# First expert's weight sums and three token groups' operand sums on VectorE, attention's buffers closed earlier, a second raw-weight buffer

## The chip, the cores and the metric

The kernel runs on one core of a Trainium2 chip. The metric is the device time of one execution in microseconds; lower is better. The core has a matrix engine (PE in the profile, TensorE), a vector engine (DVE, VectorE), an activation engine (ACT, ScalarE), a general engine (POOL, GpSimd) and a queue engine (SP, SyncE) that issues nearly all DMAs. Each engine executes its own instructions strictly in the order in which the program holds them and waits on semaphores of the others.

## The reference

Three stages follow each other. The first is a gated linear recurrence over 768 steps for 4 batches of 8 heads of width 48; the second multiplies two projections elementwise and applies two more matrices; the third is a sum over four experts, all of them applied to every token.

```python
for t in range(S):
    state = alpha[:, :, t, :, None] * state + einsum('bhd,bhe->bhde', k[:, :, t], v[:, :, t])
    y[:, :, t] = einsum('bhd,bhde->bhe', q[:, :, t], state)
x = y.transpose(0, 2, 1, 3).reshape(3072, 384)
x = ((x @ moe_w1) * (x @ moe_w2)) @ moe_w3 @ moe_w_out          # 384 -> 1024 -> 384
p = probs / (probs.sum(-1, keepdims=True) + 1e-9)
for e in range(4):
    out += p[:, e:e+1] * (relu(x @ w1[e]) @ w2[e])               # 384 -> 1024 -> 384
```

All data are float32. A float32 product is made as three PE products of two-part operands (`mm3`: high by high, low by high, high by low), so each operand exists as a rounded high half, made on ACT, and the remainder, made by a subtraction on DVE or POOL.

## The kernel before

**Attention.** 24 chunks of 128 tokens (6 steps by 4 batches), three to a tile of 384 tokens, eight tiles. Each chunk has two scans on DVE, products on DVE or POOL (`rk`, `rq`), transposes and small products on PE (`kps`, `su`, `yps`), and ends as two-part columns `xt`. The DMA called `pack` moves rows inside `xt`.

**Products** (`products(j, f)`): per tile j and 128 of the 1024 hidden columns f, nine PE products with w1 and nine with w2 (`abps`); ACT copies the first result (`a_sb`), DVE multiplies the second by it (`g_sb`), SP stores it to DRAM (`spilled`). Three PSUM banks serve these and the next step.

**Second projection** (`moe(j)`): SP loads `spilled` into eight buffers `gg`, ACT and DVE split it, and 72 PE products (`xps`) with the folded matrix w3·w_out follow. ACT puts the results into `raw_x`: tiles 2t and 2t+1 make one of four token groups t, in two buffers used in turn.

**Operands of the experts.** The experts' first product runs in a fast block scheme that makes 20 block products of sums in place of 24: the three by two blocks of x become 17 operands (`X_SUMS`, 13 additions), the twelve weight blocks become 20 (`W_SUMS`, 19 additions of 128 columns). `prepare(t)` adds on POOL, makes the high halves on ACT (`x_hi`) and the low halves on DVE or POOL (`x_lo`). For t = 0 the results go straight to the 17 slots `xo` that the expert products read; for t = 1 and 2 they go through five staging buffers (two `stage`, three `ac`) and a DMA to DRAM (`kept`). Group 3 (`last_x`) is made on POOL during the passes 2 to 4 of the experts. `load_a(e, k)` loads half of an expert's first matrix into the one raw buffer `araw`, adds on POOL and splits in pieces of 640 columns (`W_STEPS`) on ACT and DVE into `wa`.

**Expert passes.** 32 passes i in the order expert e, token group t, half k. A pass has 19 steps g (`PARTS`) with 20 times three PE products `hps`, additions on DVE that read the PSUM banks (line 1265), rectified results split by ACT and POOL (`ho`, `ht`), and 72 products `ops` of the pass before. Pass 0 has only its own first `ops`, from step 13 on. The queue reloads a slot of `xo` right behind its last use in a token group.

**Buffers.** `open_e` closes attention's buffers and opens `araw`, one slot `xo`, one `ho` and `stage` in their place; `x_open` takes 16 slots `xo` from the buffers of w1 and w2. Both wait for the last product of tile 7. The tiles `xt` lie among attention's buffers.

**The order.** Up to the first expert pass, a planner (`Plan`) writes the order of every engine: it takes the operations with their dependencies and assumed costs, and an engine that is free takes the ready operation of the smallest due number. The table of `..._DUE` and `..._STEP` numbers ahead of it sets these. From pass 0 on the order is written out by the loop over passes and by `job` lists of (pass, step) at which a piece of background work is issued.

Of the kernel before, what the change touches and what calls it, by code (L numbers as in the profile page):

```python
# [69 lines left out]
W_STEPS = ((0, 0), (0, 5), (1, 0), (0, 10), (1, 5), (0, 15), (1, 10), (1, 15))  # L70
# [264 lines left out]
TILE_DUE = 113275  # L335
CHUNK_DUE = 43206.6
ATT_DUE = -26971.1
START_DUE = -1.29833e+12
START_STEP = 642464
NEXT_DUE = -5.7734e+11  # L340
NEXT_STEP = 9.71164e+06
LOAD_DUE = -2.1073e+12
UNIT_DUE = 11170.6
ZS_DUE = 666271
CHECK_DUE = 6.11715e+06
KT_DUE = -786.104
U_DUE = 22424.3
Z_DUE = -27633.5
M_DUE = 74534.2
KW_DUE = -24366.4  # L350
QP_DUE = -18168.3
HI_DUE = 10353.8
SC_DUE = 527168
IN_DUE = 72261.5
CONV_DUE = 1650.82
CONV_STEP = 23531.8
RAW_DUE = 85566.7
WO_DUE = 1.00473e+07
W3_DUE = 646348
W3_STEP = 3551.85  # L360
WL_DUE = 1.00421e+07
WL_STEP = 50736
XS_DUE = 6.82742e+06
XS_STEP = 10579
X_DUE = 1.40744e+06
X_STEP = 1.15509e+06
G_LEAD = 4.34505e+06
FIRST_DUE = 15730.2
# [96 lines left out]
def gated_attention_moe_kernel(tc, qT, kT, aT, vP, w1, w2, w3T, wo, probs, ew, out):  # L465
# [4 lines left out]
    with tc.manual_schedule(), root:  # L470
# [3 lines left out]
        att_s = ExitStack()  # L474
        apool = att_s.enter_context(tc.tile_pool(name="att", bufs=1, side="right"))
# [47 lines left out]
        def attention(i):  # L523
# [424 lines left out]
        def open_e():  # L948
            att_s.close()
            nonlocal epool, araw  # L950
            epool = root.enter_context(tc.tile_pool(name="e", bufs=1, side="right"))
            araw = epool.tile([128, NW, 128], F32, name="araw")
# [3 lines left out]
            stages.extend(stage[:, n] for n in range(2))  # L956

        def x_open():
            for _ in range(4):
                x = wtile([128, 4, 2, HT], F32R, "xo")  # L960
                xslots.extend(x[:, n] for n in range(4))
            stages.extend(tiles["ac"][:, n] for n in range(3))
# [16 lines left out]

        def load_a(e, k):  # L980

            for f in range(4):
                nc.sync.dma_start(out=araw[:, KD * f:KD * f + KD],
                                  in_=ew[0][e, 4 * k + f].rearrange("p (n t) -> p n t", n=KD))
# [384 lines left out]
```

## Time and profile before

| | us |
|---|---|
| Device time, median of 3 runs (lowest, highest) | 1218.36 (1217.09, 1219.22) |
| Device time of the profiled execution | 1219.27 |
| Its span, first to last instruction | 1217.5 |
| PE busy in it | 1175.2 (97%) |
| DVE busy | 844.2 (69%) |
| ACT busy | 627.5 (52%) |
| POOL busy | 538.6 (44%) |

A PE product of 384 columns is shown with some 0.34 us, but the next one starts 0.17 us later, so PE's busy share hides that it runs a little slower in some stretches than in others; how many products start in a stretch tells more. The engines' busy times in a stretch, the names of what they wait for, and the chain of work that ended last are the other views used below.

### The profile page before, as it was taken

To read this page: it belongs to the slowest core of one execution; us is meant where nothing else is said; L and a number is where in the kernel's file an instruction comes from. 1 tells how busy PE (TensorE), PEld (TensorE's weight loads), DVE (VectorE), ACT (ScalarE), POOL (GpSimd) and SP (SyncE) were. 2 spreads that over 40 slices of the span, in tenths; PEclk is the share of its full clock that TensorE was granted. 3 is DMA by queue.
4 is the path that set the end of the run, shared out by engine and by line. 5 is a ranking of instruction groups with operands and counts; after the bars stand their busy time and mean duration, and the time that the engine had idled before them with its cause. 6 is when DMAs were issued, how large, how long until landed. Compare 5 with 4: busy or idle time off the path is not lost.

```text
span 1217.5 us, 24933 instructions
## 1 busy us (share of the span) xinstructions
PE 1175.2 (97%) x9186; PEld 1148.5 (94%) x9186; DVE 844.2 (69%) x1420; ACT 627.5 (52%) x1238; POOL 538.6 (44%) x610
## 2 busy tenths in 40 slices
PE   5899999999998899999999999999999999999997
PEld 5799999999997888989999999999999999999997
DVE  8898877684158997756668666686576587566573
ACT  4555555443145665544666565566555545434432
POOL 3123222100048884884656432558434357533332
PEclk8999999999999999999999999999999999999999
DMA  8756676342254689595594785775864854844821
GB/s 321 223 176 192 201 229 184 122 160 93 68 181 139 231 301 372 229 356 192 206 336 156 274 300 176 285 282 200 331 240 174 312 192 169 315 144 155 298 79 42
DMA packets 128723, 262.86 MB, mean 216 GB/s; under 512 B 17104, under 2 KB 64720, under 8 KB 128592
## 3 DMA queue, kind: packets, MB, share of 16 engines
q1 hardware_dynamic: 127728, 259.99, 60.9%
q8 instruction: 75, 1.23, 0.4%
q10 hardware_dynamic: 864, 1.18, 0.3%
q14 instruction: 56, 0.46, 0.1%
HBM read 200.56 MB, written 58.20 MB: 213 GB/s over the span
## 4 chain that ended last, share of the span: by engine, by line
PE 85%; DVE 6%; POOL 4%; DMA 2%; issue 2%; ACT 1%; SPq 0%; DVEq 0%; POOLq 0%; ACTq 0%
PE ops L87 11%; PE ops L86 11%; PE ops L88 10%; PE hps L86 9%; PE hps L87 9%; PE hps L88 8%; PE abps L86 6%; PE abps L87 6%; PE abps L88 6%; DVE raw_x L1265 2%; POOL raw_x L966 2%; PE yps L658 2%; POOL araw L987 1%; PE yps L676 1%; PE xps L88 1%
## 5 line engine op out<-in xcount | busy, mean ns | idle before, releaser
L1265 DVE TENSOR_TENSOR raw_x<-hps,raw_x 128x384 f32<-128x384 f32 x416 | 226.8, 554 | 208.0 <-PE hps L88 197.4
L1248 POOL TENSOR_TENSOR ht<-raw_x,ht 128x384 fp32r<-128x384 f32 x227 | 240.9, 1064 | 287.6 <-ACT raw_x L1247 243.1
L87 PE MATMUL ops<-wb,ht 128*128 128x384 f32 x681 | 231.4, 340 | 0.0
L86 PE MATMUL ops<-wb,ht 128*128 128x384 f32 x681 | 230.8, 339 | 0.0
L88 PE MATMUL ops<-wb,ht 128*128 128x384 f32 x681 | 230.6, 339 | 0.0
L1246 ACT ACTIVATE ht<-raw_x 128x384 fp32r<-128x384 f32 x227 | 118.6, 522 | 215.9 <-DVE raw_x L1265 198.6
L86 PE MATMUL hps<-xo,wa 128*128 128x384 f32 x640 | 219.3, 343 | 7.8 <-DVE raw_x L1265 3.6
L87 PE MATMUL hps<-xo,wa 128*128 128x384 f32 x640 | 215.8, 337 | 0.0
L88 PE MATMUL hps<-xo,wa 128*128 128x384 f32 x640 | 215.4, 337 | 0.0
L1265 DVE TENSOR_TENSOR raw_x<-raw_x,hps 128x384 f32<-128x384 f32 x256 | 136.8, 549 | 23.2 <-PE hps L88 23.2
L1247 ACT ACTIVATE raw_x<-raw_x 128x384 f32<-128x384 f32 x256 | 134.6, 526 | 8.1
L86 PEld LDWEIGHTS hps<-xo,wa 128*128 128x128 f32 x640 | 120.4, 188 | 16.3 <-DVE raw_x L1265 9.7
L86 PEld LDWEIGHTS ops<-wb,ht 128*128 128x128 f32 x681 | 128.1, 188 | 0.0
L88 PEld LDWEIGHTS ops<-wb,ht 128*128 128x128 f32 x681 | 127.9, 188 | 0.0
L87 PEld LDWEIGHTS ops<-wb,ht 128*128 128x128 f32 x681 | 127.5, 187 | 0.0
L87 PEld LDWEIGHTS hps<-xo,wa 128*128 128x128 f32 x640 | 120.5, 188 | 0.0
L88 PEld LDWEIGHTS hps<-xo,wa 128*128 128x128 f32 x640 | 120.4, 188 | 0.0
L987 POOL TENSOR_TENSOR araw<-araw 128x128 f32<-128x128 f32 x152 | 78.4, 533 | 59.8 <-DMA araw<-in_ew_dram 45.8
L1265 DVE TENSOR_TENSOR raw_x<-raw_x 128x384 f32<-128x384 f32 x128 | 91.8, 717 | 4.4
L88 PE MATMUL xps<-gg,w3h 128*128 128x384 f32 x192 | 67.1, 349 | 8.1 <-DVE gg L793 8.1
L761 DVE TENSOR_TENSOR g_sb<-abps,a_sb 128x384 f32<-128x384 f32 x64 | 35.4, 553 | 55.4 <-PE abps L88 45.0
L757 ACT ACTIVATE a_sb<-abps 128x384 f32<-128x384 f32 x64 | 31.3, 489 | 75.7 <-PE abps L88 73.2
(127 smaller groups left out, 2278.5 us busy)
## 6 DMA issues: line engine op xcount, KB each, us to landing
xo<-kept SPq DMA_DIRECT2D x255, 384.0 KB, 6.4
partial<-ac SPq DMA_DIRECT2D x72, 192.0 KB, 1.9
ac<-partial SPq DMA_DIRECT2D x72, 192.0 KB, 6.3
spilled<-g_sb SPq DMA_DIRECT2D x64, 192.0 KB, 2.2
gg<-spilled SPq DMA_DIRECT2D x64, 192.0 KB, 3.1
kept<-stage SPq DMA_DIRECT2D x22, 384.0 KB, 3.2
c_raw<-in_w3T_dram SPq DMA_DIRECT2D x16, 512.0 KB, 3.9
raw_x<-in_w3T_dram SPq DMA_DIRECT2D x8, 1024.0 KB, 6.5
```

What stands on the lines that cost most here:

```text
L86: nc.tensor.matmul(out=ps, lhsT=lh, rhs=rh, start=first, stop=False)
L87: nc.tensor.matmul(out=ps, lhsT=ll, rhs=rh, start=False, stop=False)
L88: nc.tensor.matmul(out=ps, lhsT=lh, rhs=rl, start=False, stop=last)
L658: PE.matmul(out=r["y"][rows, p, t], lhsT=Z[rows, p], rhs=r["q"][rows, p, half], start=p == 0, stop=False)
L757: A.activation(out=us["a"], in_=us[0], func=ACTF.Copy)
L761: V.tensor_tensor(out=us["g"], in0=us[1], in1=us["a"], op=ALU.mult)
L966: G.tensor_tensor(out=r[:, dst], in0=r[:, x], in1=r[:, y], op=SIGN[op])
L987: G.tensor_tensor(out=araw[:, dst], in0=araw[:, x], in1=araw[:, y], op=SIGN[op])
L1246: A.activation(out=hh[:, 0], in_=s, func=ACTF.Relu)
L1247: A.activation(out=s, in_=s, func=ACTF.Relu)
L1248: G.tensor_tensor(out=hh[:, 1], in0=s, in1=f32(hh[:, 0]), op=ALU.subtract)
L1265: V.tensor_tensor(out=tmp[:, s], in0=ins[0], in1=ins[1], op=SIGN[op])
```

## The change

- Additions of `prepare(t)` (t = 0, 1, 2), and all low halves there, are on DVE; group 3 stays on POOL. Additions for the first expert's weights are on DVE, those of the three later experts stay on POOL, now one addition per step of a pass where five stood together.
- `xt` gets a pool of its own; `open_e` waits for attention alone, and `x_open` (which takes the buffers of w1 and w2, and that of `xt` for the second half's `wa`) for the last product of tile 7.
- All three groups pass through staging buffers and DRAM: three `ac` for t = 0 and 1, five for t = 2. Seventeen loads bring group 0 into `xo`; its stores in pass 0 are gone.
- The raw weights of a second half have a place of their own: `stage` and the end of `raw_x[1]`.
- `W_STEPS` splits in pieces of 768 and 512 columns. `last_x` takes 16 of the 19 steps of a pass.
- The whole table of due numbers is new, with separate dues for each tile of `moe` and each group of `prepare`.

```diff
-W_STEPS = ((0, 0), (0, 5), (1, 0), (0, 10), (1, 5), (0, 15), (1, 10), (1, 15))
+W_STEPS = ((0, 0, 6), (0, 6, 12), (1, 0, 6), (0, 12, 16), (1, 6, 12), (0, 16, 20), (1, 12, 16), (1, 16, 20))
...
-X_DUE = 1.40744e+06
-X_STEP = 1.15509e+06
...
+X0_DUE = 152927
+X1_DUE = 20086.3
...
+        xtp = root.enter_context(tc.tile_pool(name="xt", bufs=1, side="right"))
+        xt2 = xtp.tile([128, 2, 2, NP, TT], F32R, tag="xt", name="xt")
...
-            araw = epool.tile([128, NW, 128], F32, name="araw")
+            araws.append(epool.tile([128, NW, 128], F32, name="araw"))
...
+            araws.append(f32(stage.rearrange("p b s n -> p (b s n)")).rearrange("p (n t) -> p n t", t=128))
+            wslots.append(epool.tile([128, 2, NW, 128], F32R, name="wa"))
...
-        def x_sum(t, dst, x, y, op):
+        def x_sum(eng, t, dst, x, y, op):
             r = raw_x[t % 2]
-            G.tensor_tensor(out=r[:, dst], in0=r[:, x], in1=r[:, y], op=SIGN[op])
+            eng.tensor_tensor(out=r[:, dst], in0=r[:, x], in1=r[:, y], op=SIGN[op])
...
             for n, (dst, x, y, op) in enumerate(W_SUMS):
-                G.tensor_tensor(out=araw[:, dst], in0=araw[:, x], in1=araw[:, y], op=SIGN[op])
-                if n % 5 == 4:
-                    yield
+                (G if e else V).tensor_tensor(out=raw_a(k2, dst, dst + 1), in0=raw_a(k2, x, x + 1),
+                                              in1=raw_a(k2, y, y + 1), op=SIGN[op])
+                if e or n % 5 == 4:
+                    yield
...
-        opened = add("SP", 0.0, WL_DUE, open_e, att_all, ab_done[j])
+        opened = add("SP", 0.0, WL_DUE, open_e, att_all)
+        x_ready = add("ACT", 0.0, XA_DUE, x_open, opened, ab_done[j])
...
-                    p = add("POOL", pool(HT), due, lambda a=(t, dst, o, y, op): x_sum(*a), writer[dst], writer[o],
-                            writer[y], readers[dst], port=False)
+                    p = add("DVE", dve(HT), due, lambda a=(V, t, dst, o, y, op): x_sum(*a), writer[dst], writer[o],
+                            writer[y], readers[dst])
...
-                on = (("POOL", pool(HT), G) if t and o % 2 else ("DVE", 1.25 * dve(HT), V))
-                q = add(*on[:2], due, lambda t=t, s=dst, to=to, on=on: x_lo(on[2], t, s, to()), p, port=False)
+                q = add("DVE", dve(HT), due, lambda t=t, s=dst, to=to: x_lo(V, t, s, to()), p)
...
+                k = last_keep[m] = add("SP", 0.55, due, lambda t=t, o=o, to=to: x_keep(t, o, to()), q, kib=384)
+                if t == 0:
+                    add("SP", 0.55, XL_DUE + XL_STEP * o, lambda o=o: x_load(0, o), k, x_ready, kib=384)
...
-                job(load_a(e, 0), *((i0 - 2, g) for g in (0, 0, 0, 0, 4, 8, 11, 14)), *((i0 - 1, g) for g in (0, 1, 2, 3, 4, 5, 6, 8)))
-                job(load_a(e, 1), *((i0 - 1, g) for g in (3, 5, 5, 7, 10, 12, 14, 16)), *((i0, g) for g in (4, 5, 6, 7, 8, 9, 10, 12)))
+                for k in range(KO):
+                    job(load_a(e, k), (i0 - 4 + k, 18), *((i0 - 3 + k, g) for g in range(19)),
+                        *((i0 - 1 + k, g) for g in (1, 2, 3, 4, 5, 6, 7, 9)))
...
-                if i == 0 and g < NX:
-                    x_keep(0, g, xslots[g])
-                if 1 < i < 5:
+                if 1 < i < 5 and g not in (5, 11, 18):
                     next(background, None)
```

What the table does is seen in the order. **PE, second projection.** Before, all 576 products `xps` stand in one row behind the last `abps`; the change of one to the other is:

```order
L88 MATMUL abps<-xt,w2h 128x384
L86 MATMUL abps<-xt,w2h 128x384
L87 MATMUL abps<-xt,w2l 128x384
L88 MATMUL abps<-xt,w2h 128x384
L86 MATMUL xps<-gg,w3h 128x384
L87 MATMUL xps<-gg,w3l 128x384
L88 MATMUL xps<-gg,w3h 128x384
```

Now the first `xps` stand behind 729 of the 1152 `abps`, 153 of them in a row, and then a chunk of attention:

```order
L87 MATMUL xps<-gg,w3l 128x384
L88 MATMUL xps<-gg,w3h 128x384
L673 MATMUL yps<-rq,Z_105 64x64 x8
L673 MATMUL yps<-rq,Z_110 64x64 x8
L632 MATMUL su<-rv,kT 64x48 x8
L621 MATMUL su<-rq,rk 64x64 x16
L691 MATMUL yps<-s,rv 64x64 x16
L86 MATMUL xps<-gg,w3h 128x384
L87 MATMUL xps<-gg,w3l 128x384
```

The `xps` are spread in 14 pieces; behind attention's last product there are 216 `abps` and 144 `xps`, and the last piece, 87 `xps` behind the last `abps`, ends at the first `hps`.

**POOL before, DVE now, the first expert's weights.** `rv` and `Z` belong to attention, `araw` are the weight sums, `raw_x` with two names the operand sums. POOL before, from attention's end:

```order
L684 MEMSET rv 128x1
L987 TENSOR_TENSOR araw<-araw 128x128 x19
L966 TENSOR_TENSOR raw_x_4794<-raw_x_4794 128x384 x6
L987 TENSOR_TENSOR araw<-araw 128x128 x5
L966 TENSOR_TENSOR raw_x_4794<-raw_x_4794 128x384 x7
L987 TENSOR_TENSOR araw<-araw 128x128 x14
L972 TENSOR_TENSOR ac<-raw_x_4795,ac 128x384
```

The same weight sums now, on DVE, with `g_sb` of the products between them:

```order
L990 TENSOR_TENSOR ac<-raw_x_3840,ac 128x384
L1014 TENSOR_TENSOR araw<-araw 128x128 x5
L776 TENSOR_TENSOR g_sb<-abps,a_sb 128x384
L1014 TENSOR_TENSOR araw<-araw 128x128 x10
L776 TENSOR_TENSOR g_sb<-abps,a_sb 128x384
L1014 TENSOR_TENSOR araw<-araw 128x128 x4
L808 TENSOR_TENSOR gg<-gg 128x384 x2
L776 TENSOR_TENSOR g_sb<-abps,a_sb 128x384
```

POOL now holds no sum between attention's last chunk and pass 0. **SP around pass 0.** Before, group 0 is in its slots and is stored from them:

```order
L975 DMA kept<-ac 128x768 x2
L975 DMA kept<-xo 128x768 x17
L1006 DMA braw<-in_ew_dram 128x384 x4
L978 DMA xo<-kept 128x768 x17
L975 DMA kept<-stage 128x768 x2
```

Now it is loaded, among the last loads of `gg`:

```order
L779 DMA spilled<-g_sb 128x384
L800 DMA gg<-spilled 128x384 x3
L996 DMA xo<-kept 128x768 x2
L779 DMA spilled<-g_sb 128x384
L800 DMA gg<-spilled 128x384 x4
L996 DMA xo<-kept 128x768 x2
L800 DMA gg<-spilled 128x384
L1035 DMA braw<-in_ew_dram 128x384 x4
L996 DMA xo<-kept 128x768 x13
L1035 DMA braw<-in_ew_dram 128x384 x4
L996 DMA xo<-kept 128x768 x17
```

The first 17 rows `xo<-kept` are new; the stores of group 0 stand earlier, between the loads of `gg`.

## Rows read from the trace of the kernel before

**Rows 1.** Page, busy time of engines; page, the span in 40 slices.
```profile
PE 1175.2 (97%) x9186; PEld 1148.5 (94%) x9186; DVE 844.2 (69%) x1420; ACT 627.5 (52%) x1238; POOL 538.6 (44%) x610
...
DVE  8898877684158997756668666686576587566573
POOL 3123222100048884884656432558434357533332
```

**Rows 2.** Windows: from:to, length, busy (instructions) of PE, PEld, DVE, ACT, POOL; clock, DMA share, GB/s.
```profile
0.00:45.20 45.20, 27.53 (x674) 23.52 (x674) 37.36 (x68) 23.60 (x49) 12.66 (x17) 0.85 0.85 289
45.20:336.90 291.70, 290.64 (x3710) 282.99 (x3711) 203.67 (x327) 137.57 (x301) 51.76 (x72) 1.00 0.51 161
336.90:453.40 116.50, 106.46 (x579) 100.65 (x577) 94.92 (x100) 65.85 (x141) 89.41 (x92) 0.99 0.63 214
453.40:474.00 20.60, 18.98 (x95) 17.72 (x96) 16.93 (x30) 11.01 (x23) 9.54 (x10) 0.92 0.97 378
474.00:1217.50 743.50, 731.55 (x4133) 723.66 (x4131) 491.35 (x897) 389.46 (x724) 375.22 (x420) 1.00 0.63 229
```

**Rows 3.** Timeline of PE, products without a wait: start, duration, what.
```profile
305.77 0.33 PE L86 MATMUL abps<-xt,w1h 128*128 128x384 f32 x1
...
308.89 0.33 PE L86 MATMUL abps<-xt,w1h 128*128 128x384 f32 x1
```

**Rows 4.** Instructions of tile xps: duration ns min/median/max, first to last start us.
```profile
L86 PE MATMUL xps<-gg,w3h x192: 335/336/525, 337.0 to 452.1; 128*128 128x384 f32 x192
```

**Rows 5.** Waits of PE, 336.9 to 453.4: total us, times, longest.
```profile
PE xps L88 <- DVE gg L793: 8.1, 10, 2.0
PE xps L86 <- ACT raw_x L823: 1.3, 2, 0.9
```

**Rows 6.** Chain that ended last, 366 to 405: start, us, what (the longest pieces).
```profile
375.23 1.30 POOL raw_x L966
376.60 7.32 POOL raw_x L966 x6
```

**Rows 7.** Groups on POOL, 336.9 to 453.4: count, busy, mean ns, idle before.
```profile
L966 POOL TENSOR_TENSOR raw_x<-raw_x 128x384 f32<-128x384 f32 x39 | 48.3, 1249 | 13.9 <-ACT raw_x L823 9.8 <-DVE stage L972 1.9 <-DVE xo L972 1.0
L987 POOL TENSOR_TENSOR araw<-araw 128x128 f32<-128x128 f32 x38 | 23.4, 634 | 43.1 <-DMA araw<-in_ew_dram 41.8
```

**Rows 8.** Groups on DVE, 336.9 to 453.4.
```profile
L793 DVE TENSOR_TENSOR gg<-gg 128x384 fp32r<-128x384 f32 x56 | 56.5, 1053 | 10.5 <-ACT gg L789 10.4
L972 DVE TENSOR_TENSOR xo<-raw_x,xo 128x384 fp32r<-128x384 f32 x17 | 13.9, 837 | 7.9 <-ACT xo L969 7.8
```

**Rows 9.** Group on DVE, 210 to 336.9.
```profile
L793 DVE TENSOR_TENSOR gg<-gg 128x384 fp32r<-128x384 f32 x8 | 4.1, 551 | 0.7 <-ACT gg L789 0.7
```

**Rows 10.** Group on DVE, whole span: the two-input operation of 96 columns.
```profile
L1092 DVE TENSOR_TENSOR p_sb<-p_sb,p_sum 128x96 f32<-128x96 f32 x1 | 0.3, 257 | 0.0
```

**Rows 11.** Groups on ACT, 336.9 to 453.4: high halves into the staging buffers.
```profile
L969 ACT ACTIVATE ac<-raw_x 128x384 fp32r<-128x384 f32 x19 | 9.5, 517 | 3.3 <-POOL raw_x L966 2.1 <-DMA kept<-ac 1.0
L969 ACT ACTIVATE stage<-raw_x 128x384 fp32r<-128x384 f32 x14 | 7.2, 520 | 9.2 <-POOL raw_x L966 6.3 <-DMA kept<-stage 2.9
```

**Rows 12.** DMA issues: count, KB each, median us from issue to landing.
```profile
kept<-ac SPq DMA_DIRECT2D x20, 384.0 KB, 3.4
```

**Rows 13.** Waits of PE, 0 to 60.
```profile
PE abps L86 <- DMA xt<-xt: 2.4, 1, 2.4
...
PE abps L87 <- DVE w2l L95: 1.4, 1, 1.4
```

**Rows 14.** Waits of PE, 480 to 560.
```profile
PE hps L86 <- ACT raw_x L1263: 2.3, 3, 1.2
```

**Rows 15.** Waits of PE, 560 to the end.
```profile
PE hps L86 <- DVE raw_x L1265: 2.3, 4, 0.7
```

**Rows 16.** Chain that ended last, 820 to 841, a change of expert.
```profile
829.16 1.21 POOL araw L987 x2
```

More of the change, by code (lines that the diff above doesn't have):

```diff
@@ L334 @@
 MM = 0.174
[L335 to L364, printed above, removed]
-X_DUE = 1.40744e+06
-X_STEP = 1.15509e+06
-G_LEAD = 4.34505e+06
-FIRST_DUE = 15730.2
+TILE_DUE = 145435
+CHUNK_DUE = 72150.5
+ATT_DUE = -6421.33
+START_DUE = -731.082
+START_STEP = 42665.8
+NEXT_DUE = -2467.26
+NEXT_STEP = 3757.1
+LOAD_DUE = 10481.4
+UNIT_DUE = 18928.8
+ZS_DUE = 20051.4
+CHECK_DUE = 862129
+KT_DUE = -22247.7
+U_DUE = -9258.47
+Z_DUE = -11294.3
+M_DUE = 21097.1
+KW_DUE = -14986.1
+QP_DUE = 78185.4
+HI_DUE = -1118.42
+SC_DUE = 20341.1
+IN_DUE = -2696.97
+CONV_DUE = 576.798
+CONV_STEP = 29364.4
+RAW_DUE = 62795
+WO_DUE = 2.37049e+06
+W3_DUE = -139285
+W3_STEP = 27551
+WL_DUE = 2.5277e+06
+WL_STEP = -139182
+XS_DUE = 78249.6
+XS_STEP = 202041
+XT_DUE = -68590.4
+XT_STEP = 187420
+XU_DUE = 23006.6
+XU_STEP = 1.68451e+06
+X0_DUE = 152927
+X1_DUE = 20086.3
+X2_DUE = -3995.65
+X3_DUE = -5402.66
+X4_DUE = 601929
+X5_DUE = 174157
+X6_DUE = 931289
+X7_DUE = 2.01771e+06
+XA_DUE = 1.47361e+06
+XL_DUE = 1.12115e+07
+XL_STEP = 121092
+G_LEAD = 862071
+FIRST_DUE = 21070.3
 EARLY = 3
@@ L961, in x_open @@
                 xslots.extend(x[:, n] for n in range(4))
-            stages.extend(tiles["ac"][:, n] for n in range(3))
-        def x_sum(t, dst, x, y, op):
+            w = xtp.tile([128, 4 * NP * TT], F32R, tag="xt", name="wa")
+            wslots.append(w[:, :2 * NW * 128].rearrange("p (s n c) -> p s n c", s=2, n=NW))
+        def x_sum(eng, t, dst, x, y, op):
             r = raw_x[t % 2]
-            G.tensor_tensor(out=r[:, dst], in0=r[:, x], in1=r[:, y], op=SIGN[op])
+            eng.tensor_tensor(out=r[:, dst], in0=r[:, x], in1=r[:, y], op=SIGN[op])
         def x_hi(t, slot, to):
@@ L1026, in step @@
                     gen["g"] = load_a(0, k)
-                    for _ in range(3):
-                        next(gen["g"])
                 next(gen["g"], None)
@@ L1032, in gated_attention_moe_kernel @@
             for m in (5, 5, 5, 4):
-                prev = add("POOL", m * 0.52, due + 2, step, prev, port=False)
-            for lo, _ in W_STEPS:
-                prev = add(*(("DVE", dve(640)) if lo else ("ACT", act(640))), due + 2, step, prev)
+                prev = add("DVE", m * dve(128), due + 2, step, prev)
+            for lo, s0, s1 in W_STEPS:
+                n = 128 * (s1 - s0)
+                prev = add(*(("DVE", dve(n)) if lo else ("ACT", act(n))), due + 2, step, prev, x_ready if k else None)
             wl_last = prev
-        x_ready = None
-        kept_ops = []
+        last_keep = [None] * 3 + [opened] * 2
         def prepare(t):
+            made = 0
             writer = {s: [] for s in range(NT)}
```

56 lines of the change are left out of this document (31 added, 25 removed).

## The prediction

> **What bounds the kernel now.** I read the busy shares and the 40 slices first, then the windows by stage, then PE's waits and the chain in the windows where PE falls behind. PE is busy for 97% of the span [rows 1], so a gain can come only from stretches in which PE's products stand further apart than they can. Without a wait, 18 products take 308.89 - 305.77 = 3.12 us, 0.1733 us each [rows 3]. Against that pace the five windows [rows 2] tell where the slack is:
>
> - 45.2 to 336.9 (attention and products): PE busy 290.64 of 291.70 us. Nothing to gain, though DVE is at 70%.
> - 336.9 to 453.4 (second projection alone): 576 products `xps`, three times the 192 of [rows 4], need 576 x 0.1733 = 99.8 us and take 116.5. **16.7 us are lost here.**
> - 453.4 to 474 (pass 0): some 94 products started, 16.3 us, in 20.6 us: about 4.3 us lost, at a granted clock of 0.92.
> - 0 to 45.2: PE is busy for 27.53 us at a clock of 0.85; this is the start.
> - 474 to the end: PE busy 731.55 of 743.50 us; the waits named there are 2.3 and 2.3 us [rows 14, 15].
>
> In the second window PE waits for the low half of `gg` on DVE, 8.1 us in ten waits [rows 5]; the rest of the 16.7 us are shorter gaps and the slow clock behind them. The chain there runs through POOL [rows 6]: 39 operand sums of 1249 ns and 38 weight sums of 634 ns are 48.3 + 23.4 = 71.7 us [rows 7], and POOL is busy for 89.41 of 116.5 us [rows 2]. POOL also slows DVE: the same `gg` operation takes 551 ns while POOL rests [rows 9] and 1053 ns here [rows 8].
>
> **The change part by part.** The sum is made against the profiled execution, 1219.27 us; the median of the three runs is 0.9 us lower, so the result is brought down by that.
>
> *Sums to DVE, second projection spread.* POOL's 71.7 us of sums, and 15 low halves, leave it. On DVE the 39 operand sums take 39 x 0.551 = 21.5 us if they cost what the two-input operation of the same size costs with POOL at rest [rows 9]; a weight sum of 128 columns has no row there: it lies between 257 ns for 96 columns [rows 10] and 551 ns for 384 [rows 9], and I take 290 ns, a ninth of the way (32 of 288 columns), so 11.0 us. DVE gains back 56 x (1.053 - 0.551) = 28.1 us on `gg` [rows 8, 9] and 17 x (0.837 - 0.551) = 4.9 us on the first low halves; 15 more low halves cost it 8.3 us. Net 21.5 + 11.0 + 8.3 - 28.1 - 4.9 = about +8 us on 336 us of DVE work before pass 0 [rows 2]. The work up to pass 0 takes PE some 437 us: DVE, with 344 us, is at 79% there. PE's order is what gives the gain: `xps` no longer stand in one row at the end but in 14 pieces between products and chunks, and behind attention's last product PE still holds 216 + 144 products, 62.4 us, to cover what follows it: the raw weights' DMA, 38 sums (11 us), their splits (8 pieces, 8.0 us before) and group 2's sums and halves (30 x 0.551 = 16.5 us). So the 16.7 us can go. They will not go wholly: 153 `xps` in a row need `gg` reloaded behind themselves, as before. The first 29 us of the old row (337 to 366) had no such wait while `gg` took 551 ns on DVE, so the lower bound of what stays is 0; the upper is the 8.1 us for `gg` with the 1.3 us for `raw_x` [rows 5], 9.4. I take 3, nearer to the lower, since POOL no longer slows DVE. **-13.7 us.**
>
> *The planner's new order at the start.* One conversion moves ahead of the third chunk's scans, and `xt` of that chunk, on which the first product waits through `pack`, is one row earlier on DVE. The waits there are 2.4 us for the `xt` DMA and 1.4 us for `w2l` [rows 13]: 3.8 us either way is the bound; I take **-1 us**.
>
> *Operands of group 0 through DRAM.* 17 loads of 384 KB (6.7 MB) can start only when the last product of tile 7 has freed w1's buffers, and 87 `xps` (15.1 us) stand between that and pass 0. With the 5 last loads of `gg` and 4 of `braw` (1.8 MB) it is 8.5 MB, 22.4 us at the 378 GB/s that the window of pass 0 reached [rows 2]. Pass 0 takes one operand per step, the 13th about 7 us in, 22 us behind that last product; by then 6.9 MB must have landed, 18.2 us and a landing. It just fits. **0**, with up to +10 if the rate is the mean 229 GB/s of the last window [rows 2]: 30 us for the 13th. The stores of group 0 move under attention, where the DMA share is 0.51 [rows 2], and cost nothing there.
>
> *Pass 0 itself* is paced by DVE as before. **0.**
>
> *Passes 2 to 4.* POOL makes group 3 beside its own halves; PE waits 2.3 us there [rows 14]. The same work now stretches over 48 steps instead of 47 in a row. It takes about half: **-1.2 us**, bounds -2.3 and 0.
>
> *Changes of expert.* A change has POOL sums in its chain [rows 16], then splits on DVE; PE waits 2.3 us in four places [rows 15]. Single sums per step take POOL out of it; the splits stay and become longer pieces. **-0.8 us**, bounds -2.3 and +1.
>
> Sum: -13.7 - 1 + 0 - 1.2 - 0.8 = -16.7; 1219.27 - 16.7 - 0.9 = 1201.7, say **1202 us**.
>
> *A rule against it.* The same `gg` operation costs 0.50 us more with POOL busy for 77% of the time than with POOL at rest [rows 2, 8, 9], and in the stretch from 45.2 to 336.9 POOL is busy for 18% (51.76 of 291.7). Scaled, that is 0.12 us more for each of the 39 + 38 + 51 operations put there, 15 us of DVE time, and DVE goes from 79% to 82%: no wait for PE. The Trainium skill, SBUF — State Buffer, section "SBUF: two separate sides", says that VectorE with two SBUF inputs and GpSimd share a port pair as an exclusive lock, and that the loser blocks for the whole of the other's instruction. By that rule each meeting would cost DVE up to a whole POOL product of attention instead of a share, and attention's own `rk` and `rq` would be held up in turn; that is the second rival's mechanism.
>
> **The rivals.**
>
> *Operands late for pass 0.* For it: the loads are not covered by more than 2 us in the working above. Against it: the window of pass 0 did reach 378 GB/s. Price +5 to +10: 1207 to 1212.
>
> *DVE becomes the bound under attention.* DVE is at 89% or more in several slices of the first 200 us [rows 1], and the moved operations come on top, slowed by POOL. If half of the 16.7 us comes back as PE's waits for `g_sb` or `xt`: 1210, range 1207 to 1216. Against it: the sums come after most of the weight conversion, where DVE rested before.
>
> *Slower: staging blocks ACT.* Groups 0 and 1 now have three staging buffers instead of none and five. A high half must wait until the store three tiles back has landed: 3.4 us [rows 12] after halves of 0.52 [rows 11] and 0.55 us. ACT stands still up to 3.4 us per three tiles, 34 tiles make 11 such turns, 37 us, and behind the waiting half on ACT stand the copies `a_sb` that free PE's banks. Three banks cover 27 products, 4.7 us, so a single turn costs nothing. Once each turn costs PE over 1.5 us (16.7 / 11) the kernel is no faster; at the full 3.4 it is 37 - 16.7 = 20 us slower, 1239. Before, ACT waited for such stores 1.0 + 2.9 us in all [rows 11], and the order puts copies between most of the halves, which speaks against it.
>
> *More than forecast.* The start gives its 3.8 us and nothing stays of the stalls: 1219.27 - 0.9 - 16.7 - 3.8 - 2 = 1195.
>
> **How the numbers follow.** Forecast (1195 to 1207) 0.60; operands late 0.12; DVE bound 0.13; more than forecast 0.04; within 0.2% of before (all given back) 0.04; slower, by staging or another wait in the new order, 0.07. A measurement of this kernel can tell about 0.2%, 2.4 us, from no change. The first two rivals end below 1215.9, so faster is 0.60 + 0.12 + 0.13 + 0.04 = 0.89, cut to 0.87 because the second reaches to 1216; same 0.05, slower 0.08. The range leaves out the case below the forecast, the dearest part of the second rival and what is slower: 1195 to 1213.
>
> **What would show it.** Right: pass 0 starts near 439 us instead of 453.4; `gg` takes some 0.55 to 0.7 us on DVE; POOL nearly empty from attention's end to pass 0; PE's waits for `gg` below 3 us; no wait of `hps` for a DMA. Wrong: waits of `hps` for `xo` DMAs in pass 0 (first rival), of `abps` for `g_sb` or `a_sb` between 45 and 340 us (second and third), or a later first `abps`.

## The result and the profile after

Before: 1218.69 us (median of 4, 1217.09 to 1219.22). After: **1197.20 us** (median of 4, 1196.44 to 1198.84). The ratio is 0.9828, with a 95% interval from 0.9811 to 0.9845. The forecast of 1202 was 4.8 us too high; the range, 1195 to 1213, holds the time. The profiled execution of after took 1197.35 us against 1219.27, so 21.9 us have to be found in the two traces.

The page of after, with busy time by engine and the 40 slices of VectorE and POOL (before: [rows 1]):

```profile
PE 1167.1 (98%) x9186; PEld 1149.3 (96%) x9186; DVE 829.2 (69%) x1513; ACT 627.4 (52%) x1238; POOL 445.1 (37%) x517
...
DVE  8898788966665856667677656667666587576563
POOL 2133321010000006776744434744433655433332
```

POOL has lost 93 us, and ahead of the slice in which pass 0 starts five slices in a row stand at 0. VectorE, which took the sums over, is not busier than before (829.2 against 844.2 us): its own operations became shorter. The windows of after, the first two cut at the times of [rows 2] and the others around its own pass 0; columns are from:to, length, busy time of PE, PEld, DVE, ACT, POOL, then granted clock, DMA share and GB/s:

```profile
0.00:45.20 45.20, 27.79 (x673) 23.90 (x673) 37.76 (x64) 23.02 (x48) 13.01 (x17) 0.85 0.81 281
45.20:336.90 291.70, 290.08 (x3556) 283.45 (x3555) 230.24 (x386) 158.77 (x352) 52.87 (x68) 1.00 0.63 201
336.90:440.00 103.10, 102.29 (x735) 101.19 (x733) 64.37 (x142) 46.09 (x94) 0.26 (x4) 1.00 0.73 254
440.00:460.60 20.60, 19.13 (x105) 18.07 (x106) 13.55 (x26) 11.76 (x25) 9.09 (x9) 1.00 0.61 223
460.60:1195.50 734.90, 727.85 (x4123) 722.68 (x4121) 483.25 (x896) 387.72 (x721) 369.88 (x420) 1.00 0.63 228
```

The third window is the point. It was 116.5 us long with PE busy for 106.46 at a clock of 0.99; now PE is busy for 102.29 of 103.10. The two windows do not hold the same work, since the `xps` now start at 250 us; the stretch that can be compared runs from the first `abps` to the first `hps`, in the table below. The groups on VectorE from 230 to 440 us (count, busy time, mean ns, then idle time before) show what became of the operations of [rows 7, 8]:

```profile
L808 DVE TENSOR_TENSOR gg<-gg 128x384 fp32r<-128x384 f32 x64 | 33.5, 554 | 31.0 <-ACT gg L804 30.9
...
L984 DVE TENSOR_TENSOR raw_x<-raw_x 128x384 f32<-128x384 f32 x39 | 20.8, 554 | 2.6 <-ACT raw_x L838 2.0
...
L1014 DVE TENSOR_TENSOR araw<-araw 128x128 f32<-128x128 f32 x38 | 9.7, 289 | 2.5 <-DMA araw<-in_ew_dram 1.9
```

`gg` fell from 1053 to 554 ns, an operand sum from 1249 on POOL to 554, a weight sum from 634 to 289. Waits of PE from 60 to 440 us and from 440 to 560 us (total us, times, longest):

```profile
PE yps L691 <- POOL rv L699: 0.3, 1, 0.3
...
PE hps L86 <- DVE raw_x L1294: 1.2, 1, 1.2
PE hps L86 <- ACT raw_x L838: 0.6, 1, 0.6
```

Nothing is left of [rows 5] or [rows 14]. Only the start is worse. Waits of PE from 0 to 60 us in after:

```profile
PE yps L673 <- DVE xt L710: 6.8, 4, 2.8
...
PE yps L691 <- DVE s L683: 4.5, 3, 2.3
```

The waits of [rows 13] are gone, but the wait for `xt` is three times as long as it was in before, while that for `s` is the same. In before, same window:

```profile
PE yps L676 <- DVE s L668: 4.5, 4, 2.2
...
PE yps L658 <- DVE xt L695: 2.2, 2, 2.0
```

The first `abps` starts at 40.84 instead of 38.80 us.

Where the 21.9 us are, with a pass counted from its first `hps` product to the next pass's (60 products each; a pass without a wait takes 23.20 us):

| stretch | before | after | difference |
|---|---|---|---|
| start to first `abps` | 38.80 | 40.84 | +2.0 |
| first `abps` to first `hps` | 414.60 | 399.25 | -15.35 |
| passes 0 and 1 | 37.94 | 35.90 | -2.0 |
| passes 2 to 4 | 73.62 | 69.80 | -3.8 |
| changes of expert: passes 6 to 8, 14 to 16, 22 to 24 | 215.80 | 212.70 | -3.1 |
| last pass and end | 42.25 | 42.65 | +0.4 |

### The profile page after: what moved, and what is told of

The parts are those of the page before. It is cut to its first block, busy times and chain, and to the rows that moved or that the text cites. A ratio compares the mean times of both kernels' runs of the same rounds, so it can differ in the third digit from the quotient of the medians.

```text
span 1195.5 us, 24960 instructions
## 1 busy us (share of the span) xinstructions
PE 1167.1 (98%) x9186; PEld 1149.3 (96%) x9186; DVE 829.2 (69%) x1513; ACT 627.4 (52%) x1238; POOL 445.1 (37%) x517
## 4 chain that ended last, share of the span: by engine, by line
PE 95%; DVE 3%; DMA 1%; issue 0%; POOL 0%; SPq 0%; ACT 0%; DVEq 0%; POOLq 0%
PE ops L87 11%; PE ops L86 11%; PE ops L88 11%; PE hps L86 9%; PE hps L87 9%; PE hps L88 9%; PE abps L86 6%; PE abps L87 6%; PE abps L88 6%; PE xps L86 3%; PE xps L88 3%; PE xps L87 3%; PE yps L673 2%; PE yps L691 1%; PE wps L86 1%; PE wps L88 1%
## 5 line engine op out<-in xcount | busy, mean ns | idle before, releaser
L1277 POOL TENSOR_TENSOR ht<-raw_x,ht 128x384 fp32r<-128x384 f32 x227 | 238.1, 1051 | 274.5 <-ACT raw_x L1276 222.2
L1294 DVE TENSOR_TENSOR raw_x<-raw_x 128x384 f32<-128x384 f32 x128 | 88.6, 692 | 4.4
L1277 POOL TENSOR_TENSOR ho<-raw_x,ho 128x384 fp32r<-128x384 f32 x29 | 30.7, 1060 | 105.0 <-DMA xo<-kept 71.4
L86 PE MATMUL abps<-xt,w2h 128*128 128x384 f32 x192 | 66.0, 344 | 0.0
L86 PE MATMUL abps<-xt,w1h 128*128 128x384 f32 x192 | 65.9, 343 | 0.0
```

The costliest lines, as they stand in the source:

```text
L86: nc.tensor.matmul(out=ps, lhsT=lh, rhs=rh, start=first, stop=False)
L1277: G.tensor_tensor(out=hh[:, 1], in0=s, in1=f32(hh[:, 0]), op=ALU.subtract)
L1294: V.tensor_tensor(out=tmp[:, s], in0=ins[0], in1=ins[1], op=SIGN[op])
```

## The experiments

In the table the third column is the stretch from the first `abps` to the first `hps`, the fourth from there to the end of the span; both are of the profiled execution. Times with one run are single executions. Where the expectations say first product or expert product, the `abps` are meant; a combine is one of the additions that read the PSUM banks of the `hps`, and a turn is the step of a pass at which a piece of background work is issued.

| kernel | time, us (runs) | `abps` to `hps` | `hps` to end |
|---|---|---|---|
| before | 1218.69 (4) | 414.60 | 764.14 |
| after | 1197.20 (4) | 399.25 | 755.45 |
| after again | 1196.26 (5) | 398.83 | 755.42 |
| after, all sums on POOL | 1199.59 (4) | 402.18 | 755.57 |
| before, sums on VectorE | 1205.14 (4) | 402.28 | 762.65 |
| after, operand sums alone on POOL | 1196.56 (1) | 399.65 | 756.05 |
| after, second projection in one row | 1222.53 (1) | 418.37 | 761.73 |
| after, attention's buffers closed late | 1222.96 (1) | 401.92 | 778.30 |
| after, no steps left out in passes 2 to 4 | 1201.34 (1) | 399.56 | 759.55 |
| after, later weight sums timed three ways | 1202.13 (1) | 399.79 | 759.77 |
| after, one raw-weight buffer, old turns | 1198.42 (1) | 398.07 | 758.96 |
| after, start first | 1196.22 (5) | 400.32 | 755.31 |
| after, start first and earlier turns | 1192.73 (5) | 399.17 | 753.78 |
| after, start mixed and earlier turns | 1198.31 (4) | 403.61 | 755.02 |

### Engine or order: four kernels

**After with the sums on POOL**, every other engine's row untouched:

```diff
-                (G if e else V).tensor_tensor(out=raw_a(k2, dst, dst + 1), ...
+                G.tensor_tensor(out=raw_a(k2, dst, dst + 1), ...
-                    p = add("DVE", dve(HT), due, lambda a=(V, t, dst, o, y, op): x_sum(*a), ...
+                    p = add("DVE", dve(HT), due, lambda a=(G, t, dst, o, y, op): x_sum(*a), ...
```

> The changed kernel with its order left as it is, but the 39 operand sums of the first three groups and the 38 weight sums of the first expert emitted on POOL instead of VectorE. Theory (the spreading is the gain: the operand tiles come out between the expert products, where neither engine is waited for): first hps within 2 us of the changed kernel's 440.1, total 1197 to 1200. Rival (the engine is the gain: POOL's sums slow VectorE's low halves of gg down and end late): gg on VectorE 0.7 to 1.0 us instead of 0.55, TensorE waits of 5 to 12 us before 440, first hps at 446 to 453, total 1203 to 1211.

Measured: 1199.59 us, ratio to before 0.9841 (0.9812 to 0.9869); first `hps` 2.1 us later than after's, at 442.19, just outside the theory's 2 us. With the second projection spread, PE hardly feels POOL's sums. What it feels is one place near 400 us. Waits of PE (336 to 447) and of ACT (392 to 404), then windows with the granted clock in the third column from the end:

```profile
PE abps L86 <- ACT a_sb L772: 1.8, 1, 1.8
...
ACT wa L1026 <- POOL araw L1014: 3.9, 1, 3.9
ACT stage L987 <- DMA kept<-stage: 3.5, 1, 3.5
...
402.00:406.00 4.00, 3.15 (x11) 3.15 (x12) 4.00 (x4) 3.46 (x8) 4.00 (x3) 0.65 0.14 49
406.00:410.00 4.00, 3.65 (x19) 3.33 (x18) 4.00 (x5) 1.43 (x3) 2.66 (x3) 0.93 0.50 197
```

ACT stood 3.5 us at a high half whose staging buffer was not yet stored and 3.9 us at a piece of the first expert's weights whose sums POOL had not made; `a_sb`, which frees a bank, stood behind them, and PE waited 1.8 us. Behind that wait the granted clock was 0.65 and 0.93 in the two windows, in part the lower of its two levels (1.2 instead of 2.4 GHz): 4 x 0.35 + 4 x 0.07 = 1.7 us more. The move of the sums is the only edit taken back here: the spread order, the earlier close and the new way of the operands all stay.

**Before with the sums on VectorE**, its order and its one row of `xps` kept:

```diff
-                G.tensor_tensor(out=araw[:, dst], ...
+                (G if e else V).tensor_tensor(out=araw[:, dst], ...
-            G.tensor_tensor(out=r[:, dst], in0=r[:, x], in1=r[:, y], op=SIGN[op])
+            (V if t < NT2 - 1 else G).tensor_tensor(out=r[:, dst], in0=r[:, x], in1=r[:, y], op=SIGN[op])
```

> The kernel before, its order and its one row of xps kept, but the operand sums of the first three groups and the first expert's weight sums emitted on VectorE. Theory (spreading): the wait of xps for gg (8.1 us before) goes down by half at most, first hps at 446 to 453 (before 453.4), total 1211 to 1219. Rival (engine): gg on VectorE at 0.55 us, no wait for gg above 2 us, first hps at 441 to 444, total 1206 to 1210. Passes 3, 4, 8, 16 and 24 stay as long as before on both, since nothing of them is changed.

Measured: 1205.14 us, ratio 0.9893 (0.9867 to 0.992); first `hps` at 439.74. The theory of spreading falls: without any spreading, 12.3 of the 15.35 us are there. Group `gg` on VectorE, 336 to 440 us; PE's wait for it; and the window after that wait:

```profile
L793 DVE TENSOR_TENSOR gg<-gg 128x384 fp32r<-128x384 f32 x56 | 33.7, 621 | 5.8 <-ACT gg L789 5.6
...
PE xps L88 <- DVE gg L793: 1.1, 2, 1.0
...
406.00:410.00 4.00, 3.83 (x13) 3.52 (x14) 2.98 (x6) 2.55 (x5) 1.01 (x1) 0.67 0.87 269
```

The wait for `gg` fell from 8.1 to 1.1 us as `gg` fell from 1053 to 621 ns. Of the 3.0 us that it still lacks, 2.7 are again one short wait, 1.0 us, with a slow clock behind it: 0.67 in the window shown and 0.90 in the next, 4 x 0.33 + 4 x 0.10 = 1.7 us. Pass 0 is short as well (15.89 us, before 17.57, after 15.73), while passes 3, 4 and 8 stay long (24.38, 25.79, 25.09).

**After with the operand sums alone on POOL** (only the second edit of the first diff):

> The changed kernel with the 39 operand sums of the first three groups on POOL and the first expert's weight sums left on VectorE. Theory (with the spreading, what the sums on POOL cost came of ACT's 3.9 us wait for the weight sums, and the operand sums' engine costs nothing): first product to first hps within 0.6 us of the changed kernel's 399.25, no low granted clock between 336 and 440. Rival (the operand sums cost by themselves): 401 to 402.5 from first product to first hps, as with both on POOL (402.2), and a wait of TensorE over 1 us between 390 and 420.

Measured: 399.65 us from first `abps` to first `hps`, after 399.25. The window 336 to 440 has the full clock, though POOL is busy for 20.62 us there:

```profile
336.00:440.00 104.00, 102.56 (x735) 101.14 (x735) 61.96 (x124) 46.84 (x95) 20.62 (x21) 1.00 0.73 254
```

So, once the second projection is spread, the operand sums' engine costs nothing that one execution shows. What both kinds of sums together cost on POOL then falls, by subtraction, to the first expert's weight sums, for which ACT stood 3.9 us; a kernel with those alone on POOL was not run.

**After with the second projection in one row** (the due numbers of the eight tiles made late):

```diff
-X0_DUE = 152927
...
-X7_DUE = 2.01771e+06
+X0_DUE = 1.40744e+06
...
+X7_DUE = 9.49307e+06
```

> The changed kernel with its sums on VectorE, but the due numbers of the second projection's eight tiles made late, so that its 576 products stand in one row behind the first projection's last product, as in the kernel before. Theory (the engine of the sums and the spreading each give nearly the whole gain, and what is left over is one short wait with a low clock behind it, as in the kernel before with the sums on VectorE): first hps 2 to 4 us after the changed kernel's 440.1, with the granted clock under 0.8 for some us after a wait of xps for gg; total 1199 to 1202. Rival (the early close of attention's buffers changes this, so that one row costs nothing or much more): first hps within 1 us of 440.1, or more than 6 us after it.

Measured: first `hps` at 459.00, 18.9 us after after's and 5.6 after before's. The theory's 2 to 4 us are wrong; this is the mechanism of the prediction's third rival. Waits of PE (336 to 460) and of ACT (330 to 460); then the chain that ended last (start, us, what); then a window:

```profile
PE xps L86 <- ACT raw_x L838: 4.7, 1, 4.7
PE xps L88 <- DVE gg L808: 4.4, 3, 2.2
PE xps L86 <- ACT gg L804: 2.0, 3, 1.1
...
ACT ac L987 <- DMA kept<-ac: 19.1, 26, 2.1
...
432.93 3.53 DMA kept<-ac
...
437.69 4.46 DMA kept<-ac
...
442.67 0.48 ACT raw_x L838
...
444.00:448.00 4.00, 4.00 (x14) 4.00 (x14) 3.51 (x7) 2.63 (x6) 0.00 (x0) 0.50 0.77 304
```

All the high halves of groups 0 and 1 fall into the row of `xps`; with three staging buffers ACT waits 19.1 us for stores, the copies that free PE's banks stand behind, and after PE's 4.7 us wait the clock is at its lower level for 4 us (0.50). The waits shown are 11.1 us, and the granted clock, 0.97 from 336 to 440 us and 0.83 from 440 to 460, costs 104 x 0.03 + 20 x 0.17 = 6.5 more: 17.6 of the 18.9. The chain shows the stores behind the longest wait; that they are behind the others as well is argued. In the kernel before with VectorE's sums, whose first group needs no store, no wait of ACT for a store is among the nine longest of this stretch; that this alone lets it bear one row is argued, not shown, since early close and due numbers differ as well.

### Closing attention's buffers when attention ends

```diff
-        opened = add("SP", 0.0, WL_DUE, open_e, att_all)
+        opened = add("SP", 0.0, WL_DUE, open_e, att_all, ab_done[j])
```

> The changed kernel, but attention's buffers are closed only after the last expert product of the first projection, as in the kernel before, so that the first expert's weights and two of the five staging buffers come after it. Theory (the early close lets VectorE do the weight sums, some 19 us of VectorE and ACT work with their low halves, before the last products): these fall into the last 15 us before pass 0 and behind it, first hps at 444 to 455 instead of 440.1, total 1201 to 1212. Rival (TensorE has enough of the second projection left behind the last product to cover them): first hps within 1.5 us of 440.1, total within 1 us of 1197.2.

Measured: 1222.96 us, 11 us beyond the expected band. First `hps` comes only 2.7 us later, but pass 0 lasts 38.40 us instead of 15.73, at a mean granted clock of 0.72. Waits of PE, 440 to 480, and of ACT, 430 to 475; then DMA issues from 425 to 460 (KB each, median us to landing):

```profile
PE hps L86 <- ACT raw_x L1292: 14.9, 1, 14.9
PE hps L86 <- ACT wa L1026: 4.6, 1, 4.6
...
ACT stage L987 <- DMA kept<-stage: 15.6, 4, 11.2
...
xo<-kept SPq DMA_DIRECT2D x17, 384.0 KB, 7.9
...
araw<-in_ew_dram SPq DMA_DIRECT2D x8, 192.0 KB, 5.7
```

The raw weights are now loaded in the same 35 us as the 17 operands: a load of an operand takes 7.9 us, and the chain of waits has the second half's weights landing at 459.2. VectorE's weight sums wait for them with low halves of group 2 behind; ACT waits 11.2 us for the store of such a half, and the first copy out of PSUM, on which PE waits 14.9 us, stands behind that. The early close is what keeps these two loads apart.

### Passes 2 to 4

```diff
-                if 1 < i < 5 and g not in (5, 11, 18):
+                if 1 < i < 5:
```

> The changed kernel, but the sums and halves of the last group run at every step of passes 2 to 4 again, as in the kernel before (19 steps in a pass instead of 16). Theory (the three steps left out give the combines on VectorE room): passes 3 and 4 go from 23.20 us back to 24.3 to 25.8 each, total +2 to +4 us over the changed kernel. Rival (something else shortened them, such as VectorE's backlog of operand work carried over from the start of the passes): passes 3 and 4 stay within 0.3 us of 23.2, total within 0.6 us.

Measured: passes 3 and 4 back at 24.46 and 25.78 us (before 24.57 and 25.76), every other pass within 0.5 us of after's. The three steps left out are the whole gain there. Waits of ACT from 499 to 550 us in this kernel, and of PE from 480 to 560:

```profile
ACT stage L987 <- POOL raw_x L984: 9.1, 4, 2.7
...
PE hps L86 <- ACT raw_x L1292: 2.5, 3, 1.2
```

A high half on ACT waits for POOL's sum of the step before (9.1 us; in after 3.3), with the copy out of PSUM that PE needs behind it. The waits that PE names, 2.5 us, are less than the 3.8 us that the two passes lose: short gaps around them are not named.

### Changes of expert

**Three timings of the sums**, one for each later expert:

```diff
-                    job(load_a(e, k), (i0 - 4 + k, 18), *((i0 - 3 + k, g) for g in range(19)),
+                    late, bursts = e > 1, e != 2
+                    gs = [g for g in (0, 5, 10, 15) for _ in range(5)][:19] if bursts else range(19)
+                    job(load_a(e, k), (i0 - 4 + late + k, 18), *((i0 - 3 + late + k, g) for g in gs),
```

> The changed kernel with the weight sums of the later experts timed three ways: second expert in bursts of five at the same early pass; third expert single but one pass later, so that they end just ahead of the weights' conversion; fourth expert in bursts and late. In the changed kernel passes 8, 16 and 24 last 23.67 us each, in the kernel before 24.73, 24.74 and 24.90. Theory (the early end counts, since VectorE's low halves of the weights no longer wait for POOL): pass 8 within 0.2 us of 23.67, passes 16 and 24 at 24.2 to 25. Rival (the bursts count, since they hold VectorE's combines up): passes 8 and 24 at 24.2 to 25, pass 16 within 0.2 us of 23.67.

Measured: pass 8 (bursts, early) 23.63; pass 16 (single, late) 27.33; pass 24 (bursts, late) 23.67. Bursts cost nothing, and lateness alone does not either, against the expectation for pass 24. In pass 24 the last sum ended 0.8 us after the pass began; in pass 16 it ended 6.0 us in, after the conversion's first turn on ACT. The rows of pass 16 (POOL, then ACT) and PE's wait in it:

```profile
809.06 0.46 POOL L1014 TENSOR_TENSOR stage<-raw_x,stage 128x128 f32<-128x128 f32 x1
...
809.55 0.84 ACT L1026 ACTIVATE wa<-stage 128x768 fp32r<-128x768 f32 x1 [2.84 <-POOL stage L1014]
...
PE hps L86 <- ACT raw_x L1294: 2.4, 1, 2.4
```

The kernel before has the same wait of ACT in its pass 16, on the buffer that its halves shared:

```profile
830.40 0.74 ACT L997 ACTIVATE wa<-araw 128x640 fp32r<-128x640 f32 x1 [3.66 <-POOL araw L987]
...
839.37 0.82 DVE L995 TENSOR_TENSOR wa<-araw,wa 128x640 fp32r<-128x640 f32 x1
840.10 1.24 DVE L1265 TENSOR_TENSOR raw_x<-hps,raw_x 128x384 f32<-128x384 f32 x2
```

Its conversion then ends 18 us into the pass, and its last low half stands on VectorE right ahead of a combine that PE waits for.

**One raw buffer with the old turns:**

```diff
-            k2 = e and k
+            k2 = 0
-                for k in range(KO):
-                    job(load_a(e, k), (i0 - 4 + k, 18), ...
+                bursts = [[g for g in gs for _ in range(5)][:19] for gs in ((4, 8, 11, 14), (10, 12, 14, 16))]
+                job(load_a(e, 0), (i0 - 2, 0), *((i0 - 2, g) for g in bursts[0]), *((i0 - 1, g) for g in (0, 1, 2, 3, 4, 5, 6, 8)))
+                job(load_a(e, 1), (i0 - 1, 7), *((i0 - 1, g) for g in bursts[1]), *((i0, g) for g in (4, 5, 6, 7, 8, 9, 10, 12)))
```

> The changed kernel with one raw-weight buffer for the later experts and the sums in bursts of five at the turns of the kernel before, the second half's in the pass just ahead of its conversion. Theory (POOL's sums then end some 8 us into passes 8, 16 and 24, and ACT's conversion of the weights waits for them with the combines behind it): passes 8, 16 and 24 at 24.5 to 25 us instead of 23.67, passes 7, 15 and 23 at 23.3, total +1.5 to +3.5 us over the changed kernel. Rival (the change of experts is shorter for another reason, such as the larger pieces of the conversion): passes 8, 16 and 24 within 0.3 us of 23.67, total within 1 us.

Measured: passes 8, 16, 24 at 25.36, 24.83, 24.45; passes 7, 15, 23 at 23.3; 3.5 us more than after from first `hps` to the end (the total, 1198.42 in one execution, hides it by a first `hps` 2.4 us earlier). Pass 8 of this kernel on VectorE:

```profile
630.33 1.48 DVE L1024 TENSOR_TENSOR wa<-araw,wa 128x512 fp32r<-128x512 f32 x1
631.73 0.55 DVE L1294 TENSOR_TENSOR raw_x<-hps,raw_x 128x384 f32<-128x384 f32 x1
```

PE's longest wait for a combine in this kernel's later passes, 2.0 us, is for the one in the second line. So the second raw buffer pays by letting the conversion come early in the pass. How much of it is the sums' end and how much the later turns 4 to 12 was not taken apart.

### The start, and earlier turns

**Attention's first six chunks first:**

```diff
-START_DUE = -731.082
-START_STEP = 42665.8
-NEXT_DUE = -2467.26
-NEXT_STEP = 3757.1
+START_DUE = -1e9
+START_STEP = 642464
+NEXT_DUE = -1e8
+NEXT_STEP = 9.7e6
```

> The changed kernel with four numbers of its table so altered that the first six chunks of attention stand ahead of the weight conversion again, as in the kernel before; from the seventh chunk on every engine's row of instructions is that of the changed kernel. Theory (the later start of the first expert product, 40.8 against 38.8 us, comes of the weight conversion's instructions among the first chunks on VectorE): first product at 37.4 to 39, first hps at 437 to 438.5, total 1 to 3 us under the changed kernel's 1197.2. Rival (the start differs from execution to execution by as much as 2 us whatever the order): first product at 40 or later, total within 0.6 us of 1197.2.

Measured: first `abps` at 38.79, as the theory has it, but first `hps` at 439.11, 1.0 us ahead of after instead of 1.6 to 3: around the first `abps` PE again waits for the `xt` DMA (2.6 us) and `w2l` (1.4), the waits of [rows 13]. 1196.22 us; not to be told from after.

**The same, and the weights' conversion one turn earlier:**

```diff
-                        *((i0 - 1 + k, g) for g in (1, 2, 3, 4, 5, 6, 7, 9)))
+                        *((i0 - 1 + k, g) for g in (0, 1, 2, 3, 4, 5, 6, 8)))
```

> The kernel that puts attention's first six chunks first, and besides, the conversion of the later experts' weights at the turns 0 to 6 and 8 of a pass instead of 1 to 7 and 9. Theory (in passes 7, 8, 15, 16, 23 and 24 of the changed kernel TensorE waits four times 0.1 us for a combine that stands behind a 0.95 us low half of the weights on VectorE, which the kernel with one raw buffer, with these turns, did not show in passes 7, 15 and 23): these six passes go from 23.67 to 23.2 to 23.4 us, total 1.6 to 2.8 us under the 1196.2 of the kernel with the start alone. Rival (the waits only move to other turns): the six passes stay within 0.1 us of 23.67, total within 0.6 us of 1196.2.

Measured: 1192.73 us (1192.21 to 1196.36). Five of the six passes are at 23.35 or 23.36, one at 23.72: 1.5 us less than in after.

**After again, on the same chip:**

> The changed kernel as it is, beside the others of this group, so that differences of 1 to 3 us can be told on one chip: 1196 to 1198.5.

Measured: 1196.26 us (1195.02 to 1196.69). The medians are 3.5 us apart, but against the kernel before the ratios are 0.9797 (0.978 to 0.9814) and 0.9811 (0.9798 to 0.9825): the intervals overlap. Shown by the passes are the 1.5 us of the earlier turns; the rest lies in the first 40 us, where executions of one order differ by as much (below).

**Only three chunks first, and the earlier turns** (`START_DUE` and `START_STEP` as above, `NEXT_DUE` and `NEXT_STEP` as in after):

> As the kernel with start and turns, but only the first three chunks ahead of the weight conversion, so that the w2 low half comes earlier on VectorE. Theory (after the first product the start with six chunks first gives a part back by TensorE's waits for the low half of w2, 1.4 us, and for the packed operand, 2.6 us, which come of the conversion's late turn): the wait for the low half of w2 is gone, first hps 0.5 to 2 us ahead of that kernel's. Rival (the chunks held up by the conversion wait instead): first hps at the same time or up to 2 us later.

Measured: the wait for `w2l` is gone, but the first `hps` comes at 441.52, 4.8 us behind the kernel with six chunks first; 1198.31 us. The theory was wrong, and the rival's 2 us were too few. Of the 4.4 us more between first `abps` and first `hps`, 3.6 are in the trace one wait of PE at 58 us, 1.9 us, that the profile puts down to a weight conversion on VectorE (`c_m`), and a slow clock behind it: 0.61 in the window shown and 0.96 in the next, 4 x 0.39 + 4 x 0.04 = 1.7 us. PE's wait from 55 to 70 us, then the window:

```profile
PE abps L86 <- DVE c_m L141: 1.9, 1, 1.9
...
60.00:64.00 4.00, 3.75 (x13) 3.78 (x14) 3.41 (x4) 2.59 (x5) 1.19 (x1) 0.61 0.37 119
```

## Why the prediction held, and where its sizes were off

**Second projection and sums: -13.7 forecast, -15.35 measured.** The rows meant were right: the 16.7 us, their place, 0.55 us for an operand sum (0.554) and 290 ns for a weight sum (289). Three things were wrong. First, the 3 us of remaining stalls were not there, since `gg` was never awaited. Second, the sentence that PE's order gives the gain was wrong as a cause: either half alone gives 12.3 or 12.4 us (before with VectorE's sums, after with POOL's), since each takes away the same stall. The half of after with POOL's sums is more than the order, since all else of the change is in it; the order put alone into the kernel before was not run. The last 3 us are in each of the two traces mostly one short wait with a slow clock behind it (3.5 us seen in the one, 2.7 in the other); for them it was enough, with the order, to have the weight sums on VectorE. Third, the reading behind the lower bound: the eight `gg` of [rows 9] ran at 283 to 289 us, and those between 347 and 366 us already took 0.55 to 1.37 us. PE did not wait there although `gg` was slow.

**Why the order is needed all the same.** The prediction costed the way of group 0 through DRAM at nothing because it was covered; the run with one row, which lacks that cover, starts its passes 18.9 us later. The prediction gave this mechanism as its slower rival with an end at 1239 and the condition that each turn costs PE over 1.5 us. In after ACT waits for these stores too, 17.2 us in all between 230 and 440 us (`ac` 14.7, `stage` 2.5), but PE waits for nothing there but 0.3 us. That the `abps` between the spread `xps` keep PE fed through them is argued, not shown by itself.

**Operands late: did not happen.** There is no wait of `hps` for a DMA in pass 0. The working "it just fits" was right only with the raw weights out of the way, as the late close shows.

**VectorE the bound under attention: did not happen.** It is busy for 37.76 + 230.24 + 64.37 = 332.4 of 440 us, 76%, where the prediction had 79%. It argued for this rival from several slices at 89% or more; [rows 1] show one slice at 90% or more in the first 200 us.

**Start: -1 forecast, +2.0 measured.** The prediction saw that one conversion moves ahead of the third chunk's scans on VectorE, but counted only the waits of [rows 13], which did go, and put the chunks' delay behind it at nothing: the wait for `xt` grew from 2.2 to 6.8 us.

**Pass 0: 0 forecast, -1.8 measured.** The prediction noted a granted clock of 0.92 there, took the pass as paced by VectorE's combines and gave the clock no term. The waits of PE that the profile names in it are alike in both kernels, 1.2 us for a combine and 0.6 for a copy (and 0.3 more in before). What differs is the clock. Windows of pass 0 in before, of its slowest 2 us, and of pass 0 in after:

```profile
453.40:471.00 17.60, 15.98 (x79) 14.93 (x80) 16.73 (x30) 8.62 (x18) 7.32 (x8) 0.90 0.96 375
...
466.00:468.00 2.00, 2.00 (x8) 2.00 (x7) 1.70 (x4) 1.04 (x2) 0.39 (x1) 0.50 1.03 399
...
440.10:455.80 15.70, 14.32 (x78) 13.49 (x79) 12.75 (x25) 7.95 (x16) 5.93 (x6) 1.00 0.64 247
```

17.6 x 0.10 = 1.8 us, which is the difference. The kernel before with VectorE's sums has the same short pass 0, at a clock of 1.00, with the same 1.2 us wait. Why the clock fell behind that wait in before and not in these two is open.

**Passes 2 to 4: -1.2 forecast, -3.8 measured**, outside its bound of -2.3. **Changes of expert: -0.8 forecast, -3.1 measured**, bound -2.3. Both were sized by the waits that PE names ([rows 14, 15]); the lengths of the passes, which the trace of before held as well, give 4.0 us for passes 2 to 4 above 23.20 each, and 7.0 us for the nine passes of the changes. The place and mechanism of the first were right; in the second POOL's sums were rightly blamed, but what they delay is ACT's conversion in the pass that follows.

**The total.** It came within 4.8 us in part by luck: four gains were put too low by 8.4 us together (1.65, 1.8, 2.6 and 2.3), and the start, put 3.0 us too good, hides a part of that. The sum of the last rival, 1219.27 - 0.9 - 16.7 - 3.8 - 2, is 1195.9 and not 1195.

## What to carry to other kernels

Size a stall by how much longer a repeated stage takes than its undisturbed copies; the named waits held only about 60% of what was lost in passes 2 to 4. Before crediting one of two edits that remove the same stall, run each alone: here either gave four fifths of the gain, and one of them, the order, seems to have its worth in covering a third edit. On an engine that works in order, place a step only behind the end of what it needs, since all that stands behind it waits too.

## What the runs showed of the hardware

**An operand in PSUM spares VectorE the meeting with POOL.** After with POOL's sums, VectorE from 403 to 408 us, and POOL's row beside it, six operand sums in 7.89 us:

```profile
403.46 0.54 DVE L776 TENSOR_TENSOR g_sb<-abps,a_sb 128x384 f32<-128x384 f32 x1
...
405.14 1.35 DVE L990 TENSOR_TENSOR stage<-raw_x,stage 128x384 fp32r<-128x384 f32 x1
...
400.77 7.89 POOL L984 TENSOR_TENSOR raw_x<-raw_x 128x384 f32<-128x384 f32 x6
```

The operation with one input in PSUM keeps its 0.54 us, as do all ten `g_sb` of this run that POOL's operations cover nearly wholly (0.54 to 0.56); one of the same size with both inputs in SBUF takes 1.35. The Trainium skill, SBUF — State Buffer, section "SBUF: two separate sides", says that VectorE with two SBUF inputs and GpSimd hold the shared ports in turn, each for a whole instruction; the trace agrees that both lose, with 0.8 us added to 0.55, and 7.89 / 6 = 1.32 us for a sum on POOL that takes 1.02 in the kernel without left-out steps (499 to 545 us). Two whole turns one after the other would be 0.55 + 1.02 = 1.57 us, so a lock for the full length shown is not borne out. In the kernel after, POOL is empty there and the rule has nothing to act on from attention's end to pass 0.

**A short wait can cost as much again in the clock.** PE's waits of 1.8 us (clock 0.65 in the 4 us that follow, after with POOL's sums), 1.0 us (0.67, before with VectorE's sums) and 4.7 us (0.50, one row) were each followed by a drop toward the lower of its two levels; after has no wait over 0.6 us between 60 and 440 us, and a clock of 1.00. But not each such wait is followed by one. Behind the wait of some 1.2 us for a combine in pass 0, which all fourteen profiles have, the clock fell in two (before, and one row) and stayed at 1.00 in the other twelve; a wait of 2.0 us in pass 8 of the kernel with one raw buffer had no drop behind it either. What decides is open.

**The start differs from execution to execution.** Nine executions whose first instructions stand in after's order had the first `abps` at 38.79 to 40.89 us (mean 40.3); four with before's order at 37.46 to 38.80 (mean 38.15). A difference of 1 us at the start cannot be read from one trace.
